# Attention of batches 2 to 7 and the states' expert rounds laid piece by piece between the batches' expert products

## The chip, the cores and the metric

The kernel runs on one core of a Trainium2 chip. Its time is the device time of one execution in microseconds (us), the median over runs. Engines are named as the profile names them: PE (TensorE), PEld (its weight loads), DVE (VectorE), ACT (ScalarE), POOL (GpSimd), SP (SyncE, which here issues loads and stores).

## The reference

Eight batches of eight heads: 512 tokens and 32 state vectors a head, 64 wide. Attention goes both ways, the tokens read the states and the states read the tokens; the two results are joined to 4352 rows of 512, and each row goes through one of eight experts, the one that its logits choose.

```python
# x (8, 8, 512, 64), state (8, 8, 32, 64), fp32
scores = scale * np.matmul(x, state.transpose(0, 1, 3, 2))       # softmax over the 32 states
xread = np.matmul(a, state)
scores2 = scale * np.matmul(state, x.transpose(0, 1, 3, 2))      # softmax over the 512 tokens
sread = np.matmul(a2, x)
attn_out = np.concatenate([xread, sread], axis=2)                # (8, 8, 544, 64)
x = attn_out.transpose(0, 2, 1, 3).reshape(B * S, H * D)         # (4352, 512)
logits = x @ w_gate                                              # w_gate (512, 8)
expert_idx = np.argmax(logits, axis=1)                           # gate_w: softmax at that index
for e in range(E):                                               # w1 (8, 512, 1024), w2 (8, 1024, 512)
    mask = expert_idx == e
    h = np.maximum(x[mask] @ w1[e], 0.0)
    out[mask] = gate_w[mask, None] * (h @ w2[e])
```

## The kernel before

All products are in fp32, which the profile shows as two passes each. The kernel has three parts in program order.

**Attention, batch by batch.** `load_x(b)` loads the tokens of a batch (three buffers `x_nat`). `transpose_x` transposes them in four groups of four through a PSUM buffer of pool `ps_m` (two buffers), each group copied to `xT` by ACT. `prep_state` (L161) transposes the states out of `bd`, a zeroed tile into which eight loads put the states block by block, into `stT`, and multiplies them with the gate weights (`pg`, to `gst`). `scores` (L183) makes `pc` (four products of 512 columns, pool `ps_c`, two buffers). `read_weights` (L191) is the softmax over the states: transpose, maximum, difference on DVE, exponential on ACT, sum and reciprocal on DVE, the scaling on POOL (L204), transpose back into `aT` on DVE (L205). `write_weights` is the softmax over the tokens: row maximum `nm` on DVE, two exponentials with sums on ACT. `transpose_write` and `write_rows` (L231) make the states' own rows (`pw`) and store them to DRAM with four small transfers that ACT issues. `logits_x` (L248) makes the tokens' logits (`pl`). The tokens' rows are never formed: `aT` stands for them.

**Routing.** `route` finds each row's expert and gate weight, `choose` (L292) the expert that most tokens of a batch want (`eb`). Batches 0 and 1 are routed after batch 1's attention, and their weights loaded then (`load_w1` L317 with one buffer, `load_w2` L321 with two); batches 2 to 7 and the states' rows are routed after the last batch. The 256 states' rows are sorted by expert into 16 groups of 32 rows, scattered to `ss_dram` by POOL at their place `slot_i` (L391, L395), and `eg` holds the expert of each group.

**Experts.** For a batch, `states_w1` (L442) multiplies the states with the expert's W1 (`pG`, to `G`), `up` (L455) applies the attention weights (`ph`, 8 x 2 products, then a relu to `hT`), and `down` (L467) multiplies with W2 in four chunks of rows (`py`, 4 x 8 products), scales them by the gate weight and stores them. So one expert serves a whole batch; tokens that want another are mended at the end under `tc.If(n_left > 0)`. The states' rows go through four **rounds** of four groups: `round_in` loads the rows (`xg`) and reads the experts' numbers into registers of SP, `round_w1` and `round_w2` load weight tiles of 1 MB by four transfers (three buffers each, `s1`, `s2`), `round_x` transposes the rows (`ptx`), `round_up` makes `pgh`, `round_h` the relu and transposes (`pth`), `round_down` makes `pgy`, `round_out` scales and scatters to the result. Half a round goes with each batch: a piece of it stands after each of the four chunks of `down`.

The source gives the order of dependent work; the framework's scheduler then lays out the order on each engine. Each engine runs its own queue strictly in that order, and SP's transfers are one such queue: a transfer that waits for a buffer holds up those behind it. All stores of the result's token rows are on SP. PSUM pools are released and allocated anew between attention and experts (L413 on), so that `ps_h` has three buffers, `ps_y` two, `ps_g` two, `ps_t` one in the second part.

```python
    for b in range(B):
        a2, s2 = soft
        if b + 2 < B:
            load_x(b + 2)
        if b + 1 < B:
            soft = weights(b + 1)
        a2T = transpose_write(a2)
        write_rows(b, a2T, s2)
        logits_x(b)
```

Of the kernel before, what the change touches and what calls it, by code (L numbers as in the profile page):

```python
# [9 lines left out]
FP32 = mybir.dt.float32  # L10
# [10 lines left out]
def kernel(  # L21
# [13 lines left out]

    nc = tc.nc
# [3 lines left out]
    DM = H * D  # L40
# [13 lines left out]
    NR = NG // 4  # L54
    FAR = 1 << 20
# [73 lines left out]

    att = tc.alloc_tile_pool(name="att", bufs=2)  # L130
    ps_c = tc.alloc_tile_pool(name="ps_c", bufs=2, space=PSUM)
    ps_m = tc.alloc_tile_pool(name="ps_m", bufs=2, space=PSUM)
    ps_o = tc.alloc_tile_pool(name="ps_o", bufs=1, space=PSUM)
# [3 lines left out]
    bd = att.tile([128, B, 2, 4, D], FP32, bufs=1)  # L137
    nc.gpsimd.memset(bd[:], 0.0)
    for i in range(4):
        for g in range(2):  # L140
            nc.scalar.dma_start(out=bd[ts(i, NS), :, g, i, :],
                                in_=state[:, 4 * g + i].rearrange("b n d -> n b d"))
# [18 lines left out]
    def prep_state(b):  # L161
        pt = ps_m.tile([128, 2, 2, 128], FP32, tag="m", name="pt")
        for j in range(NPR):
            nc.tensor.transpose(pt[:, j // 2, j % 2, :], bd[:, b, j // 2, ts(j % 2, 2), :], ident[:])  # L164
        for i in range(2):
            evict(stT[:, b].rearrange("p (g i) n -> p g i n", i=2)[:, :, i, :], pt[:, :, i, ts(i, 2 * NS)])

        pg = ps_s.tile([128, 2, E], FP32, tag="s", name="pg")
        for j in range(NPR):
            nc.tensor.matmul(pg[ds(64 * (j % 2), 64), j // 2, :], lhsT=stT[:, b, j, :], rhs=wg[:, j, :],  # L170
                             start=True, stop=True, skip_group_check=True)
        evict(gst[:, b], pg[:])

    def transpose_x(b):
        xT = att.tile([128, NPR, NC, 128], FP32, tag="xT", name="xT")
        for j in range(NPR):
            pt = ps_m.tile([128, NC, 128], FP32, tag="m", name="pt")
            for c in range(NC):
                nc.tensor.transpose(pt[:, c, :], x_nat[b][:, c, ts(j, 2), :], ident[:])  # L179
            nc.scalar.copy(xT[:, j], pt[:])  # L180
        return xT
# [49 lines left out]
    def write_rows(b, a2T, s2):  # L231


        pw = ps_o.tile([128, 2, 2, D], FP32, tag="o", name="pw")
# [90 lines left out]
    def weights(b):  # L325
        xT = transpose_x(b)
        prep_state(b)
        pc = scores(b, xT)
        read_weights(b, pc)
        return write_weights(pc)  # L330
# [3 lines left out]
    soft = weights(0)  # L334
    for b in range(B):
        a2, s2 = soft
        if b + 2 < B:
            load_x(b + 2)
        if b + 1 < B:
            soft = weights(b + 1)  # L340
        a2T = transpose_write(a2)
        write_rows(b, a2T, s2)
        logits_x(b)
        if b == 1:
            route(0, 2 * NC)
            choose(0, 2)
            for i in range(2):
                e = expert_of(eb, i)
                if i == 0:
                    load_w1(0, e)  # L350
                load_w2(i, e)
    logits_s()
    route(2 * NC, (B - 2) * NC + NST)
    choose(2, B - 2)
# [57 lines left out]
    for pool in (ps_s, ps_o, ps_m, ps_c, att):  # L412
        pool.release()  # L413


    ffn = tc.alloc_tile_pool(name="ffn", bufs=2)
    ps_h = tc.alloc_tile_pool(name="ps_h", bufs=3, space=PSUM)
    ps_y = tc.alloc_tile_pool(name="ps_y", bufs=2, space=PSUM)
    ps_g = tc.alloc_tile_pool(name="ps_g", bufs=2, space=PSUM)
    ps_t = tc.alloc_tile_pool(name="ps_t", bufs=1, space=PSUM)  # L420

    def no_dep(d):
        tc.declare_no_dep(d.ins, group="y", reason="every row of the result is written once")
        tc.add_to_no_dep_group("y", d.ins)

    def relu(dst, src):
        turn[0] += 1
        if turn[0] % 2:
            nc.scalar.activation(dst, src, AF.Relu)  # L429
        else:  # L430
            nc.vector.tensor_scalar(dst, src, 0.0, None, ALU.max)  # L431

    def scaled(dst, src, by):
        turn[0] += 1
        if turn[0] % 2:
            nc.scalar.activation(dst, src, AF.Copy, scale=by)  # L436
        else:
            nc.vector.tensor_scalar(dst, src, by, None, ALU.mult)  # L438

    gs, hs = {}, {}  # L440

    def states_w1(w1t, st):  # L442

        G = ffn.tile([128, 2, F], FP32, tag="G", bufs=1, name="G")
        for g in range(2):
            for k in range(2):
                pg = ps_h.tile([128, 512], FP32, tag="h", name="pG")
                for i in range(2):
                    j = 2 * g + i
                    nc.tensor.matmul(pg[ts(i, 64), :], lhsT=st[:, j, :], rhs=w1t[:, j, ts(k, 512)],  # L450
                                     start=True, stop=True, skip_group_check=True)
                evict(G[:, g, ts(k, 512)], pg[:])
        return G

    def up(G, a, insert=None):  # L455
        hT = [ffn.tile([128, S], FP32, tag="hT", bufs=12, name="hT") for _ in range(NFC)]
        for f in range(NFC):
            ph = ps_h.tile([128, S], FP32, tag="h", name="ph")
            for g in range(2):
                nc.tensor.matmul(ph[:], lhsT=G[:, g, ts(f, 128)], rhs=a[:, g, :],  # L460
                                 start=(g == 0), stop=(g == 1))
            relu(hT[f][:], ph[:])
            if insert:
                insert(f)
        return hT

    def down(hT, w2t, store, insert=None):  # L467
        for c in range(NC):
            py = ps_y.tile([128, DM], FP32, tag="y", name="py")
            for f in range(NFC):  # L470
                nc.tensor.matmul(py[:], lhsT=hT[f][:, ts(c, 128)], rhs=w2t[:, f, :],  # L471
                                 start=(f == 0), stop=(f == NFC - 1))
            store(c, py)
            if insert:
                insert(c)

    def store_batch(b):
        rows = out[ds(b * SO, S)].rearrange("(p c) f -> p c f", c=NC)

        def store(c, py):  # L480
            y = ffn.tile([128, DM], FP32, tag="y", bufs=3, name="y")
            scaled(y[:], py[:], gw[:, NC * b + c, :])
            no_dep(nc.sync.dma_start(out=rows[:, c], in_=y[:]))
        return store
# [4 lines left out]
    def round_in(r):  # L489
        xg = ffn.tile([128, XW], FP32, tag="xg", name="xg")  # L490
        nc.sync.dma_start(out=xg[:].bitcast(I32), in_=ss_dram[ts(r, 128)])
        rd[r].update(xg=xg, e=[expert_of(eg, 4 * r + q) for q in range(4)])

    def round_w1(r, k, half):
        t = ffn.tile([128, 4, 512], FP32, tag="s1", bufs=3, name="s1")
# [5 lines left out]
    def round_w2(r, f):  # L501
        t = ffn.tile([128, 4, DM], FP32, tag="s2", bufs=3, name="s2")
# [5 lines left out]
    def round_x(r):  # L508
# [3 lines left out]
        xT = ffn.tile([128, NDC, 128], FP32, tag="sxT", name="sxT")  # L512
        evict(xT[:], pt[:])
        rd[r]["xT"] = xT
        rd[r]["ph"] = [ps_g.tile([128, 512], FP32, tag="g", name="pgh") for _ in range(2)]
# [8 lines left out]
    def round_h(r):  # L524
        h = ffn.tile([128, F], FP32, tag="sh", bufs=1, name="sh")
        for half in range(2):
            relu(h[:, ts(half, 512)], rd[r]["ph"][half][:])
        hT = ffn.tile([128, NFC, 128], FP32, tag="shT", bufs=1, name="shT")
# [5 lines left out]
        rd[r].update(hT=hT, py=ps_g.tile([128, DM], FP32, tag="g", name="pgy"))  # L534
# [7 lines left out]
    def round_out(r):  # L542
        xg = rd[r]["xg"]
        y = ffn.tile([128, DM], FP32, tag="y", bufs=3, name="ys")
        scaled(y[:], rd[r]["py"][:], xg[:, DM:DM + 1])
# [3 lines left out]

    G = states_w1(w1s[0], stT[:, 0])  # L550
    e_next = expert_of(eb, 1)
    load_w1(1, e_next)
    round_in(0)
    hT = up(G, aT[:, 0])
    for b in range(B):
        r = b // 2
        if b % 2 == 0:
            round_x(r)
            for k in range(NDC):
                for half in range(2):  # L560
                    round_w1(r, k, half)
        else:
            round_h(r)
            for f in range(NFC):
                round_w2(r, f)
            if r + 1 < NR:
                round_in(r + 1)
        if b + 1 < B:
            G = states_w1(w1s[b + 1], stT[:, b + 1])
        if b + 2 < B:  # L570
            e = expert_of(eb, b + 2)
            load_w1(b + 2, e)
            load_w2(b + 2, e)

        def insert(c):
            if b % 2 == 0:
                round_up(r, c)
            else:
                round_down(r, 2 * c)
                round_down(r, 2 * c + 1)  # L580
        down(hT, w2s[b], store_batch(b), insert)
        if b % 2:
            round_out(r)
        if b + 1 < B:
            hT = up(G, aT[:, b + 1])
# [71 lines left out]
    for pool in (ps_t, ps_g, ps_y, ps_h, ffn):  # L657
        pool.release()
# [30 lines left out]
```

## Time and profile before

| what | us |
|---|---|
| median of three runs | 604.9 (603.94 to 605.38) |
| the profiled execution | 603.11 |
| its span | 601.3 |
| PE busy in the span | 544.4 |
| DVE, ACT, POOL busy | 137.5, 97.9, 26.9 |
| loads of the rounds' weights (s) | 256 of 256 KB |
| loads of w1t and w2t | 8 and 8 of 2048 KB |

The page divides the span into 40 slices of 15 us and gives the busy share of each engine in tenths, the clock that TensorE was granted, and the share of the 16 DMA engines. Products appear with the name of their PSUM tile first (`py<-w2t,hT` is a product into `py`). The costliest groups on PE are `py` (512 passes, 228.4 us), `ph` (256, 113.1), `pG` (128, 35.7), `pgh` and `pgy` (256 each, 30.8 each) and `pc` (64, 28.1); passes overlap in the array, so that their mean durations (599 ns for py) are longer than the time from one to the next, which a chain of many passes shows. The chain of waits follows the work that ended last back to its start; a stretch ("windows") gives sums between two times.

### The profile page before, as it was taken

The page shows a single profiled execution, that of the slowest core. Times are in us where ns is not written, and L with a number is a line of the kernel's source. Part 1 is how long each engine was busy: PE and PEld are TensorE (multiplying, and loading weights), DVE is VectorE, ACT ScalarE, POOL GpSimd, SP SyncE. Part 2 cuts the span into 40 slices and gives each one's busy share as a digit, 9 for nine tenths or more (in the row PEclk, how much of TensorE's full clock was granted, in tenths as well). Part 3 has the DMA queues.
Part 4 walks back from the last instruction along what each step waited for, and adds up shares of the span by engine and source line. Part 5 has one row for each costly group of instructions (what it writes and reads, how often), then busy time and mean ns, then how long its engine had stood idle before and what let it go on. Part 6 is the DMA issues. An engine that isn't in the chain of part 4 may idle for free.

```text
span 601.3 us, 6244 instructions
## 1 busy us (share of the span) xinstructions
PE 544.4 (91%) x2229; PEld 248.0 (41%) x2229; DVE 137.5 (23%) x255; ACT 97.9 (16%) x185; POOL 26.9 (4%) x30
## 2 busy tenths in 40 slices
PE   3796768769499999999999999999999999999996
PEld 1455546536243344334333433443343334334432
DVE  3368455544421012001100200120011002001100
ACT  1444324132111011001101100110011012001100
POOL 3021001111010000000000000000000000000000
PEclk9987878688599999999999999999999999999999
DMA  9333964000076897479488926965891888486173
GB/s 216 99 75 82 374 165 114 3 4 9 19 258 218 268 320 265 157 259 367 162 252 311 345 87 255 365 231 195 274 391 68 284 301 311 137 250 242 34 282 107
DMA packets 94513, 122.63 MB, mean 204 GB/s; under 512 B 43791, under 2 KB 43791, under 8 KB 94480
## 3 DMA queue, kind: packets, MB, share of 16 engines
q1 hardware_dynamic: 88160, 119.04, 60.0%
q10 hardware_dynamic: 5840, 2.12, 1.5%
q0 software_dynamic: 480, 1.05, 0.4%
q8 instruction: 18, 0.29, 0.2%
q14 instruction: 15, 0.12, 0.1%
HBM read 111.17 MB, written 11.54 MB: 204 GB/s over the span
## 4 chain that ended last, share of the span: by engine, by line
issue 54%; PE 30%; DVE 6%; DMA 3%; POOL 2%; ACT 2%; ACTq 1%; SPq 0%; POOLq 0%
PE py L471 9%; PE ph L460 5%; PE pc L187 4%; PE pG L450 2%; PE pw L238 2%; PE pl L252 2%; POOL sx L204 2%; DMA bd<-in_state_dram 1%; PE pgy L538 1%; ACTq L245 1%; PE pgh L520 1%; DVE aT L205 1%; PE pt L227 1%; DVE sm L201 1%; PE pg L170 1%
## 5 line engine op out<-in xcount | busy, mean ns | idle before, releaser
L471 PE MATMUL py<-w2t,hT 128*128 128x512 f32 x512 | 228.4, 599 | 0.0
L471 PEld LDWEIGHTS py<-w2t,hT 128*128 128x128 f32 x512 | 94.7, 190 | 132.4 <-issue 132.4
L460 PE MATMUL ph<-aT,G 128*128 128x512 f32 x256 | 113.1, 600 | 0.0
L460 PEld LDWEIGHTS ph<-aT,G 128*128 128x128 f32 x256 | 48.5, 192 | 65.4 <-issue 59.0
L438 DVE TENSOR_SCALAR y<-py,gw 128x512 f32<-128x512 f32 x16 | 12.0, 750 | 258.4 <-PE py L471 241.3
L436 ACT ACTIVATE y<-py,gw 128x512 f32<-128x512 f32 x16 | 11.0, 687 | 195.3 <-PE py L471 195.3
L431 DVE TENSOR_SCALAR hT<-ph 128x512 f32<-128x512 f32 x32 | 22.1, 691 | 88.5 <-PE ph L460 88.5
L450 PE MATMUL pG<-w1t,stT 128*64 128x512 f32 x128 | 35.7, 625 | 1.6 <-ACT G L125 1.6
L429 ACT ACTIVATE hT<-ph 128x512 f32<-128x512 f32 x32 | 19.1, 597 | 89.0 <-PE ph L460 89.0
L179 PE MATMUL pt<-ident,x_nat 128*128 128x128 f32 x128 | 21.2, 309 | 12.8 <-ACT xT L180 6.9
L520 PE MATMUL pgh<-s,sxT 128*32 128x512 f32 x256 | 30.8, 598 | 0.0
L538 PE MATMUL pgy<-s,shT 128*32 128x512 f32 x256 | 30.8, 598 | 0.0
L187 PE MATMUL pc<-xT,stT 128*64 128x512 f32 x64 | 28.1, 895 | 0.0
L179 PEld LDWEIGHTS pt<-ident,x_nat 128*128 128x128 f32 x128 | 15.6, 155 | 18.3 <-ACT xT L180 9.0
L546 POOL DMA_INDIRECT out_dram<-ys,xg x4 | 3.9, 980 | 426.4 <-ACT ys L436 318.1
L180 ACT COPY xT<-pt 128x512 f32<-128x512 f32 x32 | 17.5, 590 | 24.1 <-PE pt L179 14.0
L204 POOL TENSOR_TENSOR sx<-sx,sm 128x1024 f32<-128x1024 f32 x8 | 15.3, 1911 | 123.0 <-DVE sm L203 105.5
L164 PE MATMUL pt<-ident,bd 128*128 128x128 f32 x32 | 7.1, 360 | 13.9 <-DMA bd<-in_state_dram 7.6
L170 PE MATMUL pg<-wg,stT 128*64 128x8 f32 x64 | 7.0, 248 | 13.0 <-DVE stT L127 12.7
L238 PE MATMUL pw<-x_nat,a2T 128*64 128x128 f32 x256 | 17.2, 284 | 0.0
L238 PEld LDWEIGHTS pw<-x_nat,a2T 128*64 128x64 f32 x256 | 15.0, 142 | 2.7 <-issue 2.6
L450 PEld LDWEIGHTS pG<-w1t,stT 128*64 128x64 f32 x128 | 9.4, 140 | 16.2 <-issue 14.2
(117 smaller groups left out, 285.8 us busy)
## 6 DMA issues: line engine op xcount, KB each, us to landing
s<-in_moe_w_dram SPq DMA_DIRECT2D x256, 256.0 KB, 5.0
w1t<-in_moe_w_dram SPq DMA_DIRECT2D x8, 2048.0 KB, 9.5
w2t<-in_moe_w_dram SPq DMA_DIRECT2D x8, 2048.0 KB, 11.1
x_nat<-in_x_dram SPq DMA_DIRECT2D x32, 256.0 KB, 4.1
out_dram<-y SPq DMA_DIRECT2D x32, 256.0 KB, 3.0
ss_dram<-blank ACTq DMA_DIRECT2D x4, 257.0 KB, 4.4
xg<-ss_dram SPq DMA_DIRECT2D x4, 257.0 KB, 5.5
bd<-in_state_dram ACTq DMA_DIRECT2D x8, 64.0 KB, 3.9
```

The costliest lines, as they stand in the source:

```text
L179: nc.tensor.transpose(pt[:, c, :], x_nat[b][:, c, ts(j, 2), :], ident[:])
L180: nc.scalar.copy(xT[:, j], pt[:])
L187: nc.tensor.matmul(pc[ts(j % 2, 64), j // 2, :], lhsT=stT[:, b, j, :], rhs=xT[:, j], start=True, stop=True, skip_group_check=True)
L204: nc.gpsimd.tensor_tensor(sx[:], sx[:], sm[:].to_broadcast([128, NB, NS]), ALU.mult)
L238: nc.tensor.matmul(pw[ts(i, 64), g], lhsT=a2T[:, g, c, ts(i, 64)], rhs=x_nat[b][:, c, ts(2 * g + i, 2), :], start=(c == 0), stop=(c == NC ...
L429: nc.scalar.activation(dst, src, AF.Relu)
L431: nc.vector.tensor_scalar(dst, src, 0.0, None, ALU.max)
L450: nc.tensor.matmul(pg[ts(i, 64), :], lhsT=st[:, j, :], rhs=w1t[:, j, ts(k, 512)], start=True, stop=True, skip_group_check=True)
L460: nc.tensor.matmul(ph[:], lhsT=G[:, g, ts(f, 128)], rhs=a[:, g, :], start=(g == 0), stop=(g == 1))
L471: nc.tensor.matmul(py[:], lhsT=hT[f][:, ts(c, 128)], rhs=w2t[:, f, :], start=(f == 0), stop=(f == NFC - 1))
L520: nc.tensor.matmul(rd[r]["ph"][half][ts(q, 32), :], lhsT=rd[r]["xT"][:, k, ts(q, 32)], rhs=rd[r][1, k, half][:, q, :], start=(k == 0), sto ...
L538: nc.tensor.matmul(rd[r]["py"][ts(q, 32), :], lhsT=rd[r]["hT"][:, f, ts(q, 32)], rhs=rd[r][2, f][:, q, :], start=(f == 0), stop=(f == NFC ...
```

## The change

The pools of the expert part (`ffn`, `ps_h`, `ps_y`) are allocated before attention, so that both parts can stand side by side; PSUM is shared out anew: `ps_h` two buffers, `ps_y` two, `ps_c` one, `ps_m` one, `ps_s` one (`pw` uses it too). Later `ps_g` has two and `ps_t` one.

The attention of a batch is cut into pieces, as Python generators: `front(b)` yields after each of the four transpose groups, after `prep_state`, and after scores and softmax; `back(b)` yields after the transposes of the write weights, after `write_rows`, after `logits_x`. `run` advances `front(b + 1)` and `back(b)` in step, and `finish(b)` routes: batch 0, batch 1 and batch 2 alone, 3 and 4 after batch 4, 5 to 7 and the states' rows after batch 7. Attention of batches 0 and 1 runs in front; from then on `up` and `down` call `piece()` after each of the eight chunks of `up` and after each pair of products of `down`, first for the attention of batches 2 to 7 (in the expert products of batches 0 and 1 and the `up` of batch 2), then, from the `down` of batch 2 on, for the four rounds.

```diff
+    S1B, S2B = 4, 3
...
-    bd = att.tile([128, B, 2, 4, D], FP32, bufs=1)
-    nc.gpsimd.memset(bd[:], 0.0)
-    for i in range(4):
-        for g in range(2):
-            nc.scalar.dma_start(out=bd[ts(i, NS), :, g, i, :],
-                                in_=state[:, 4 * g + i].rearrange("b n d -> n b d"))
+    st2 = att.tile([128, B * 2, 2, D], FP32, bufs=1)
+    st_rows = state.rearrange("b (g i) n d -> (i n) (b g) d", g=2)
+    for u in (slice(0, 2), slice(2, 2 * B)):
+        for k in range(2):
+            nc.scalar.dma_start(out=st2[:, u, k, :], in_=st_rows[:, u])
+    nc.vector.memset(stT[:], 0.0)
...
     def prep_state(b):
-        pt = ps_m.tile([128, 2, 2, 128], FP32, tag="m", name="pt")
-        for j in range(NPR):
-            nc.tensor.transpose(pt[:, j // 2, j % 2, :], bd[:, b, j // 2, ts(j % 2, 2), :], ident[:])
+        pt = ps_m.tile([128, 2, 2, 2, NS], FP32, tag="m", name="pt")
+        for g in range(2):
+            nc.tensor.transpose(pt[:, g], st2[:, 2 * b + g], ident[:])
         for i in range(2):
-            evict(stT[:, b].rearrange("p (g i) n -> p g i n", i=2)[:, :, i, :], pt[:, :, i, ts(i, 2 * NS)])
+            evict(stT[ts(i, 64), b].rearrange("p (g j) n -> p g j n", g=2)[:, :, :, ts(i, NS)],
+                  pt[ts(i, 64), :, :, i, :])
...
+    def front(b):
+        xT = att.tile([128, NPR, NC, 128], FP32, tag="xT", bufs=1, name="xT")
+        for j in range(NPR):
+            transpose_x(b, xT, j)
+            yield
+        prep_state(b)
+        yield
+        pc = scores(b, xT)
+        soft[b] = write_weights(pc)
+        read_weights(b, pc)
+        yield
+
+    def back(b):
+        yield
+        yield
+        yield
+        a2, s2 = soft[b]
+        a2T = transpose_write(a2)
+        yield
+        write_rows(b, a2T, s2)
+        if b + 3 < B:
+            load_x(b + 3)
+        yield
+        logits_x(b)
+        yield
+
+    def finish(b):
+        b0, nb = {0: (0, 1), 1: (1, 1), 2: (2, 1), 4: (3, 2), B - 1: (5, 3)}.get(b, (0, 0))
+        if b == B - 1:
+            logits_s()
+        if nb:
+            route(b0 * NC, nb * NC + (NST if b == B - 1 else 0))
+            choose(b0, nb)
...
+    def attention(b0, b1):
+        yield from front(b0)
+        for b in range(b0, b1):
+            yield from run(*([front(b + 1)] if b + 1 < b1 else []), back(b))
+            finish(b)
...
     def up(G, a, insert=None):
-        hT = [ffn.tile([128, S], FP32, tag="hT", bufs=12, name="hT") for _ in range(NFC)]
+        hT = [ffn.tile([128, S], FP32, tag="hT", bufs=NFC, name="hT") for _ in range(NFC)]
...
     def down(hT, w2t, store, insert=None):
         for c in range(NC):
             py = ps_y.tile([128, DM], FP32, tag="y", name="py")
             for f in range(NFC):
                 nc.tensor.matmul(py[:], lhsT=hT[f][:, ts(c, 128)], rhs=w2t[:, f, :],
                                  start=(f == 0), stop=(f == NFC - 1))
+                if insert and f % 2 and f + 1 < NFC:
+                    insert()
             store(c, py)
...
         def store(c, py):
             y = ffn.tile([128, DM], FP32, tag="y", bufs=3, name="y")
-            scaled(y[:], py[:], gw[:, NC * b + c, :])
-            no_dep(nc.sync.dma_start(out=rows[:, c], in_=y[:]))
+            nc.scalar.activation(y[:], py[:], AF.Copy, scale=gw[:, NC * b + c, :])
+            no_dep(nc.scalar.dma_start(out=rows[:, c], in_=y[:]))
...
+    for _ in attention(0, 2):
+        pass
+    e0 = expert_of(eb, 0)
+    load_w1(0, e0)
+    load_w2(0, e0)
+    load_w2(1, expert_of(eb, 1))
+    work = attention(2, B)
...
+    def batch(b):
+        nonlocal G, hT
+        if b + 1 < B:
+            G = states_w1(w1s[b + 1], stT[:, b + 1])
+            if 0 < b and b + 2 < B:
+                load_w1(b + 2, expert_of(eb, b + 2))
+        down(hT, w2s[b], store_batch(b), piece)
+        if b + 2 < B:
+            e = expert_of(eb, b + 2)
+            if b == 0:
+                load_w1(b + 2, e)
+            load_w2(b + 2, e)
+        if b + 1 < B:
+            hT = up(G, aT[:, b + 1], piece)
+
+    G = states_w1(w1s[0], stT[:, 0])
+    load_w1(1, expert_of(eb, 1))
+    hT = up(G, aT[:, 0], piece)
+    batch(0)
+    batch(1)
+    for _ in work:
+        pass
...
+    def fetch(n1, n2):
+        for _ in range(n1):
+            if need1:
+                round_w1(*need1.pop(0))
+        for _ in range(n2):
+            if need2:
+                round_w2(*need2.pop(0))
+
+    def rounds():
+        round_in(0)
+        fetch(S1B, S2B)
+        for r in range(NR):
+            round_x(r)
+            yield
+            if r + 1 < NR:
+                round_in(r + 1)
+            yield
+            for k in range(NDC):
+                round_up(r, k)
+                fetch(2, 0)
+                yield
+                yield
+                yield
+            round_h(r)
+            yield
+            for f in range(NFC):
+                round_down(r, f)
+                fetch(0, 1)
+                yield
+                yield
+            round_out(r)
+
+    work = rounds()
+    for b in range(2, B):
+        batch(b)
+    for _ in work:
+        pass
```

The rounds' weight tiles have four (`s1`) and three (`s2`) buffers; `need1` and `need2` list them in order of use, and `fetch` asks for the next ones as a piece releases theirs. The scaling of the rounds' rows (`round_out`) is put on DVE alone.

## The prediction

> **What bounds the kernel now.** I read the page's forty slices first, then the sums by stretch, then the chain of waits, then the timelines of SP and POOL. The slices:
>
> ```profile
> PE   3796768769499999999999999999999999999996
> PEclk9987878688599999999999999999999999999999
> DMA  9333964000076897479488926965891888486173
> ```
>
> From slice 12 on (15 us each) TensorE is full at full clock; before it, it is a half to nine tenths busy at a lower clock, and in slices 8 to 11 the DMA engines do nothing. The stretches say how far apart the two halves are (columns: stretch, its length, busy us and instructions of PE, PEld, DVE, ACT, POOL, granted clock, DMA share, GB/s):
>
> ```profile
> 72.00:164.50 92.50, 63.48 (x458) 44.70 (x458) 46.09 (x100) 26.30 (x57) 9.55 (x5) 0.77 0.25 65
> 164.50:597.00 432.50, 431.56 (x1442) 170.38 (x1440) 52.67 (x77) 46.35 (x75) 5.07 (x5) 1.00 0.71 243
> 220.00:225.00 5.00, 5.00 (x13) 2.23 (x12) 0.77 (x2) 0.97 (x2) 0.00 (x0) 1.00 1.03 393
> 275.00:280.00 5.00, 5.00 (x13) 2.20 (x12) 0.85 (x2) 0.88 (x2) 0.98 (x1) 1.00 1.03 385
> ```
>
> The second stretch can only shrink by fewer products. The first is a chain, one batch after another (chain of waits, start, us, what):
>
> ```profile
> 60.23 3.51 PE pc L187 x7
> ...
> 64.60 1.90 PE pw L238 x32
> 66.50 1.88 PE pl L252 x16
> ...
> 72.36 1.23 DVE sm L201
> ...
> 74.33 1.92 POOL sx L204
> 76.27 1.25 DVE aT L205
> 77.52 0.19 DVE stT L127
> ```
>
> Scores, softmax through VectorE, ScalarE and GpSimd, and only then the next batch's state copy and scores: aT L205 ends at 77.5 and at 110.5 two batches later, 16.5 us a batch here, 18.3 for the next (128.8). The later stage goes at these rates:
>
> ```profile
> 179.55 0.44 PE ptx L511 x4
> 179.99 3.58 PE pG L450 x16
> 183.57 7.06 PE py L471 x16
> 190.63 1.85 PE pgh L520 x16
> ...
> 219.24 13.93 PE ph L460 x32
> ```
>
> **What the change removes: the exposed attention of batches 2 to 7.** I price TensorE's work behind the first product with W1 (pG), at full clock. Experts and rounds: py 512 x 0.441 = 225.9; ph 256 x 0.435 = 111.4; pG 128 x 0.224 = 28.7; pgh and pgy 512 x 0.116 = 59.3; 48 transposes of rounds x 0.11 = 5.3; sum 430.6. (The stretch above has 431.6, so the rates hold.) In the built program's order, what stands behind the first pG of attention is batches 4 to 7 whole, batch 3 from its last score product on and batch 2's pw and pl: 64 transposes of x, 40 of weights, 8 of states at 0.11 = 12.3; pc 34 x 0.224 (its shape is pG's) = 7.6; pw 6 x 1.90 = 11.4; pl 6 x 1.88 = 11.3; pg 4 x 0.5 = 2.0; the states' logits and counts 3.8. Sum 48.4, together **479.0**.
>
> The clock is part of this: pc takes 0.50 a pass in the chain (3.51/7), where the clock is 0.77, and pG of the same shape 0.224 at 1.00.
>
> **Where the products start.** The same order puts them behind batch 3's first three score products. Walk: x of batch 0 has landed at 7.3 as now. With one buffer for transposes in place of two, each group goes 0.54 for four transposes, 0.58 for the copy (L180) and two handoffs of 0.2: 1.5, so the fourth copy ends near 13; the states wait no longer for the 3.5 us memset (L138) and its eight loads (18.0 now), so states 1, pg 0.5 and eight score passes at 0.5 end at 18 (now 23.7). Softmax 0 takes its 13.9 (23.7 to 37.6 now) plus about 1.5, as the row maximum and its wait for two exponentials now stand ahead of the transpose on VectorE; the scores of batch 1 end at 35.5. Softmax 1 with batch 0's routing in its queue: 15.5, so 51. Batch 2's scores stand on TensorE behind batch 1's logits (1.9) and around its count (route 2): 58.5. Then six transpose groups 9.0, exponential and state 1.6, three score pairs at the cold 0.49 x 6 = 2.9: **72**. Expert 0 is known at about 50 (57.9 now) and its 2 MB take 9.5 (w1t, page), so weights do not set this start. If the softmaxes overlap better 66, if every handoff doubles 78.
>
> **What it adds behind the start.**
> - Cold first products: now ph's first 32 take 15.0 against 13.9, and 162.5 to 164.5 has clock 0.50. I take 2.5 (1 to 3.5).
> - Two buffers for pG and ph, where there were three: an eviction (0.59 or 0.69) and two handoffs just exceed a pG group of 0.9. 0.2 x 8 = 1.5 (0 to 4). If ScalarE is late, ph waits too; that is in the next term.
> - Attention among products. Per batch there are seven pieces between products of 4 x 0.441, 12.3, and 8.9 of its own, 21.2 us of TensorE, against the chain's 17 or so plus the evictions, relus and the y scaling now in the same queues (1 to 5 us). It nearly fits. Nothing in this trace shows such a mixture. Lower bound 0 (TensorE has more work than the chain is long), upper 14 (5 us late, less 2, times five batches). 6, nearer to the row of 17.
> - The states' last rows: their load now stands on SP behind batch 3's w2 (2 MB). TensorE has 9 us of ph to cover 8.7; 1 (0 to 2).
> - The rounds' start. Now the scatter, the first rows and the first weights are hidden under 15 us of ph:
>
> ```profile
> 165.40 1.14 POOL L395 DMA_INDIRECT ss_dram<-srow,slot_i  x1 [20.92 <-DVE slot_i L391]
> ...
> 174.19 0.34 SPq L491 DMA_DIRECT2D xg<-ss_dram  x1
> 175.04 8.54 SPq L497 DMA_DIRECT2D s<-in_moe_w_dram  x12
> ```
>
> The place index is ready at 165.1, the rows' load is issued 9.1 later, weights 9.9 later, and four loads of 256 KB need about 2 to issue and 5.0 to land: 17. In the changed order only eleven py (9.7) and two short pieces (1.3) stand in between, and SP's weights are queued behind the waiting rows. 17 + 0.9 - 11 is **7** (3 to 9).
> - Weights in the rounds. Between the first ptx and the last pgy TensorE has 286 us of work (same sums). In it go 67.1 MB of s, 16.8 of w1t and w2t, 7.3 of outputs: 91 MB, 318 GB/s. The rows above reach 385 to 393, so 236 us would do, but leads are short: three s2 tiles have 7 us between the release of their buffer and their use, against 2 + 5 to issue and land; the input of round 3 waits on SP for round 1's scatter and a 2 MB w2 stands ahead of its weights. 5 (0 to 18).
> - The y stores move from SP to ScalarE's queue. Their loads (0.35 each on SP) leave SP; on ScalarE a store waits for its y and, in the built program, for an earlier transfer that shares its semaphore, and relus queue behind it. TensorE's py and ph buffers cover about 2 us; without that each late transfer would show whole. Counted in the 5.
> - All y on ScalarE, ys on VectorE, state loads of two instead of eight shapes, the memset of stT: nothing, since 0.69 per 7 us of py hides the first two, and the memset ends (1.8, half of the 3.5 of L138) before the first state copy at 13. Uncovered, that memset would cost 1.8 once.
> - The tail: now the last product ends at 596.1 and the span at 601.3, with an indirect store last. Then y (0.7), issue and landing 3.0: 4.5 (4 to 5).
>
> **The sum.** 72 + 479.0 + 2.5 + 1.5 + 6 + 1 + 7 + 5 + 4.5 = 578.5 of span. The profiled execution took 603.1 against its span of 601.3, so 580.3; the median of the runs is 1.8 above that execution, which makes **582**.
>
> The Trainium skill, "TensorE: Matmul & The Clock Gate", part 1 on the clock gate, says that idling longer than some 3.4 us returns the array to half clock for about as long again; the rows agree with half clock (0.50 against 0.224 a pass). By it the 7 us wait at the rounds' start costs 1.7 more and the total were 584. The skill's "DMA: Bandwidth & Descriptors", section on the specifications, speaks against the change's denser loading: it limits a core to about 358 GB/s from HBM. The rows of 385 and 393 deny it, and by it 91 MB would take 254 us, still under 286, with the same sum.
>
> **Rivals.**
> - *The gaps close* (0.18): handoffs overlap as in the later stage today (431.6 busy of 432.5). Start 66, terms 1, 0.5, 1, 0, 3, 1, tail 4.3: 555.8 + 3.6 = 559. Against it: the first stage today idles at one buffer more.
> - *The softmax chain sets the pace* (0.14): 25 us a batch against 21.2, five batches, 19 instead of 6: 595, with a late start 601. For it: stT of the next batch stands behind aT on VectorE, in the new order too. Against: TensorE has more work than the chain's 17.
> - *Loading sets the rounds' pace* (0.15, slower): place, the weights of the rounds with four and three buffers and one in-order SP. At 270 GB/s, between 243 over the stage now and 318 asked, 91 MB take 337, so 51 in place of 5: 628. It decides below 91/(286 + 5 + 23) = 290 GB/s. For it: a short lead, and a late load holds up all behind it. Against: 385 and 393 in stretches of weights alone.
> - *The moved work isn't overlapped* (0.03): the order still runs attention in front, 603 to 607. The order speaks against it.
>
> **Numbers.** The forecast, 570 to 596, has 0.50. About 0.2% is what a measurement tells from no change. Faster: 0.50 + 0.18 + 0.13 = 0.81; same 0.03; slower 0.16. The range for 8 in 10, 558 to 610, leaves out half of the first rival and most of the third.
>
> **What would show it.** pG of batch 0 first at 66 to 78 and not behind a w1 load; py, ph at 0.441 and 0.435 with attention between; pc at about 0.22 a pass; slices near 9 from the fifth on; one gap of 3 to 9 at the first ptx; DMA over 300 GB/s in the rounds, with idle on TensorE before pgh or pgy under 10 us in all. I am wrong if TensorE's idle behind the start exceeds 43 us (20.5 in the sum and the 23 that are lacking to 605), or if its products slow down.

## The result and the profile after

The changed kernel is slower: 642.94 us median (642.71 to 645.0) against 604.42 (602.91 to 605.38), a ratio of 1.065 with a 95% interval of 1.062 to 1.068. Its profiled span is 640.8 us. The prediction said 582, with 558 to 610 as its range.

The page's slices after (16 us each here):

```profile
PE   1778699999999999799999999999999999999997
PEclk9996799999999999999999999999999999999999
DMA  9433930376131044976985879677697779635501
```

The picture is the one that was predicted. From the sixth slice on TensorE is full at full clock, but for the slice in which the rounds start, where before it was so from the twelfth or thirteenth. The sums by stretch (length; busy us and count of PE, PEld, DVE, ACT, POOL; granted clock; DMA share; GB/s) say how full, first for the attention among products, then for the rounds:

```profile
81.00:240.00 159.00, 156.96 (x765) 81.33 (x763) 62.65 (x123) 44.81 (x89) 10.85 (x6) 1.00 0.34 106
270.00:636.00 366.00, 364.50 (x1124) 114.55 (x1121) 28.59 (x41) 37.53 (x60) 3.91 (x4) 1.00 0.69 236
```

TensorE idles 2.0 us in the first and 1.5 in the second. So hardly anything waits, and yet the kernel is slower: the work itself has grown. The costliest groups show where (tile, passes | busy us, mean ns of one):

```profile
L429 PE MATMUL py<-w2t,hT 128*128 128x512 f32 x512 | 241.8, 606 | 0.0
L418 PE MATMUL ph<-aT,G 128*128 128x512 f32 x256 | 123.3, 609 | 0.0
L581 PE MATMUL pgh<-s,sxT 128*32 128x512 f32 x256 | 60.3, 602 | 0.0
L599 PE MATMUL pgy<-s,shT 128*32 128x512 f32 x256 | 59.5, 604 | 0.0
```

The rounds' products in the kernel before:

```profile
L520 PE MATMUL pgh<-s,sxT 128*32 128x512 f32 x256 | 30.8, 598 | 0.0
L538 PE MATMUL pgy<-s,shT 128*32 128x512 f32 x256 | 30.8, 598 | 0.0
```

pgh and pgy were busy 30.8 us each and are now busy 60.3 and 59.5, with the same 256 passes each and the same mean duration. Only the time from one to the next can have changed. Two stretches of TensorE's timeline, before and after (start, length, what, how many passes; a product in fp32 is two passes). Before:

```profile
183.50 7.13 PE L471 MATMUL py<-w2t,hT 128*128 128x512 f32 x16
190.56 1.93 PE L520 MATMUL pgh<-s,sxT 128*32 128x512 f32 x16
192.42 7.13 PE L471 MATMUL py<-w2t,hT 128*128 128x512 f32 x16
```

After:

```profile
265.51 1.05 PE L581 MATMUL pgh<-s,sxT 128*32 128x512 f32 x2
266.49 1.13 PE L429 MATMUL py<-w2t,hT 128*128 128x512 f32 x2
267.54 1.04 PE L581 MATMUL pgh<-s,sxT 128*32 128x512 f32 x2
268.52 1.12 PE L429 MATMUL py<-w2t,hT 128*128 128x512 f32 x2
...
317.01 2.78 PE L599 MATMUL pgy<-s,shT 128*32 128x512 f32 x22
319.72 2.84 PE L418 MATMUL ph<-aT,G 128*128 128x512 f32 x6
```

Before, eight products of pgh stand together, and from their start to the next py is 1.86 us: 0.116 a pass. After, one product (x2) stands between two of py, and a pair of one pgh and one py takes 267.54 - 265.51 = 2.03 us. The py alone is 2 x 0.441 = 0.88, so the lone pgh adds 1.15 us, 0.58 a pass. The last two lines show the same kind of product still at 0.123 a pass (2.71 us from the first to the next product) where eleven stand together. A pgh or pgy product fills 32 of the array's 128 columns (the shape `128*32`), its quarter given by q; four quarters side by side share the time of one full pass, and a full-width product between them seems to end that.

In the changed kernel's order on TensorE, pgh and pgy stand in 101 runs between full-width products: 41 of one product, 28 of two, 8 of three, 15 of four, 8 of eight and one of eleven. Before there were 32 runs of eight. The source suggests why: each weight tile comes by four transfers, one a quarter, so that the scheduler can expect a quarter's product ahead of its neighbours' and fill up with py. No run here tests that; what follows tests the order itself.

### The profile page after: what moved, and what is told of

Read it like the earlier page. It is cut to its first block, busy times and chain, and to the rows that moved or that the text cites. A ratio compares the mean times of both kernels' runs of the same rounds, so it can differ in the third digit from the quotient of the medians.

```text
span 640.8 us, 6269 instructions
## 1 busy us (share of the span) xinstructions
PE 600.3 (94%) x2225; PEld 235.7 (37%) x2225; DVE 131.6 (21%) x287; ACT 108.9 (17%) x202; POOL 23.4 (4%) x29
## 4 chain that ended last, share of the span: by engine, by line
PE 85%; issue 6%; ACT 4%; DMA 3%; DVE 2%; ACTq 1%; SPq 0%; POOL 0%; POOLq 0%
PE py L429 33%; PE ph L418 16%; PE pgh L581 9%; PE pgy L599 8%; PE pG L408 4%; PE pc L193 4%; PE pt L186 3%; PE pw L244 2%; PE pl L258 2%; PE pt L233 1%; DMA st<-in_state_dram 1%; ACT xT L187 1%; DMA ss_dram<-srow,slot_i 1%; ACT a L221 1%; PE pth L593 1%
## 5 line engine op out<-in xcount | busy, mean ns | idle before, releaser
L429 PE MATMUL py<-w2t,hT 128*128 128x512 f32 x512 | 241.8, 606 | 0.0
L418 PE MATMUL ph<-aT,G 128*128 128x512 f32 x256 | 123.3, 609 | 0.0
L581 PE MATMUL pgh<-s,sxT 128*32 128x512 f32 x256 | 60.3, 602 | 0.0
L442 ACT ACTIVATE y<-py,gw 128x512 f32<-128x512 f32 x32 | 22.0, 687 | 224.2 <-PE py L429 200.6
L599 PE MATMUL pgy<-s,shT 128*32 128x512 f32 x256 | 59.5, 604 | 0.0
L186 PE MATMUL pt<-ident,x_nat 128*128 128x128 f32 x128 | 26.3, 333 | 20.7 <-ACT xT L187 12.1
L581 PEld LDWEIGHTS pgh<-s,sxT 128*32 128x32 f32 x256 | 9.4, 108 | 42.0 <-issue 32.8
L599 PEld LDWEIGHTS pgy<-s,shT 128*32 128x32 f32 x256 | 8.6, 108 | 37.7 <-issue 33.1
L258 PEld LDWEIGHTS pl<-gst,aT 128*128 128x128 f32 x128 | 15.2, 194 | 5.8 <-issue 5.3
L233 PE MATMUL pt<-ident,a 128*128 128x128 f32 x64 | 12.0, 319 | 4.2 <-ACT a2T L234 2.0
```

The source lines that it names most:

```text
L258: nc.tensor.matmul(pl[:, c, :], lhsT=aT[:, b, g, ts(c, 128)], rhs=gst[:, b, g, :], start=(g == 0), stop=(g == 1), skip_group_check=True)
L442: nc.scalar.activation(y[:], py[:], AF.Copy, scale=gw[:, NC * b + c, :])
L581: nc.tensor.matmul(rd[r]["ph"][half][ts(q, 32), :], lhsT=rd[r]["xT"][:, k, ts(q, 32)], rhs=rd[r][1, k, half][:, q, :], start=(k == 0), sto ...
L599: nc.tensor.matmul(rd[r]["py"][ts(q, 32), :], lhsT=rd[r]["hT"][:, f, ts(q, 32)], rhs=rd[r][2, f][:, q, :], start=(f == 0), stop=(f == NFC ...
```

## Experiments

**Grouped.** The changed kernel with the four quarters of a group kept together, the one that is loaded last first:

```diff
+    def together(one):
+        last = one(3)
+        with tc.issue_after(last.ins):
+            for q in range(3):
+                one(q)
...
-            for q in range(4):
-                nc.tensor.matmul(rd[r]["ph"][half][ts(q, 32), :], ...)
+            def one(q):
+                return nc.tensor.matmul(rd[r]["ph"][half][ts(q, 32), :], ...)
+            together(one)
```

> The changed kernel with one edit: the four products of a quarter group (pgh or pgy, q = 0 to 3) are issued with nothing between them, q = 3 first. In the changed kernel its 512 pgh and pgy passes are busy 119.8 us, in the kernel before 61.6. Theory (the loss is the overlap of the four quarter-width products, which ends where a full-width product stands between them): one run of such products between full-width ones takes about 1.15 us whether it holds one or two (period 2.03 us for one pgh and one py, less 0.88 for the py), and at most 1.15 for four; 39 runs of four, 5 shorter or longer and 9 of eight to twelve make 61 to 71 us, so 49 to 58 us go and the time is 585 to 594. Rival (the loading of the rounds' weights or the y stores on ScalarE's queue hold the products up, and the longer pgh only shows the wait): the time stays above 630. Rival (half and half: with the stage 50 us shorter the same 67 MB of weights don't come in time): 600 to 625, with idle before pgh and pgy over 10 us.

Measured: 593.27 us, 0.983 of the kernel before (0.979 to 0.987). 49.7 us are gone, and the sign of the change is turned by the order of 256 products alone. Its groups:

```profile
L581 PE MATMUL pgh<-s,sxT 128*32 128x512 f32 x256 | 33.6, 601 | 3.1 <-DMA s<-in_moe_w_dram 3.1
L600 PE MATMUL pgy<-s,shT 128*32 128x512 f32 x256 | 37.0, 603 | 1.6 <-DMA s<-in_moe_w_dram 1.6
```

119.8 us have become 70.6, 49.2 less; the time follows to within 0.5. The rivals wanted over 630, or 600 to 625 with more than 10 us of idle before these products; there are 4.7.

**Ones, twos and fours.** The other direction: the kernel before, with nothing changed but where its rounds' products stand. `PIECE` is 1, 2 or 4:

```diff
             for f in range(NFC):
                 nc.tensor.matmul(py[:], lhsT=hT[f][:, ts(c, 128)], rhs=w2t[:, f, :],
                                  start=(f == 0), stop=(f == NFC - 1))
+                if insert and f % PIECE == PIECE - 1:
+                    insert(c, f + 1 - PIECE, f + 1)
             store(c, py)
-            if insert:
-                insert(c)
```

> The kernel before, its rounds' products laid one by one behind each py product, in place of eight behind eight py; loads, buffers and everything else as before. Theory (a full-width product between quarter-width ones ends their overlap): 256 runs of 1.15 us in place of 32 of 1.85: 294 less 59, 235 us more, 840 us (800 to 860). Rival (the changed kernel's loss comes from loading or queues): the work is the same and the time stays within 590 to 620.

> As the run of ones, with two rounds' products behind every two py. Theory: 128 runs of 1.15 (two quarters still overlap each other): 147 less 59, 88 us more, 692 us (670 to 710). If two quarters in a row did not overlap, 840 as with ones. Rival (loading or queues): 590 to 620.

> As the run of ones, with four rounds' products (one whole quarter group) behind every four py. Theory: 64 runs of 0.93 to 1.15 us: 60 to 74 less 59, 0 to 15 us more, 604 to 620. It tells whether a single group of four already has the full overlap or needs a second group behind it. Rival (loading or queues): no change, 600 to 608, here not told apart from the lower end.

Measured: ones 841.29 us, 1.393 of before (1.383 to 1.404); twos 686.71, 1.137 (1.132 to 1.143); fours 613.75, 1.017 (1.013 to 1.022). All three lie where the theory put them, and 237 us appear in a kernel whose loads, queues and buffers are as they were. Timelines of ones, of twos and of fours:

```profile
201.88 1.04 PE L522 MATMUL pgh<-s,sxT 128*32 128x512 f32 x2
202.85 1.12 PE L472 MATMUL py<-w2t,hT 128*128 128x512 f32 x2
203.91 1.04 PE L522 MATMUL pgh<-s,sxT 128*32 128x512 f32 x2
```

```profile
201.61 1.98 PE L472 MATMUL py<-w2t,hT 128*128 128x512 f32 x4
203.52 1.05 PE L522 MATMUL pgh<-s,sxT 128*32 128x512 f32 x4
204.51 1.98 PE L472 MATMUL py<-w2t,hT 128*128 128x512 f32 x4
```

```profile
205.16 1.07 PE L522 MATMUL pgh<-s,sxT 128*32 128x512 f32 x8
206.15 3.70 PE L472 MATMUL py<-w2t,hT 128*128 128x512 f32 x8
209.78 1.06 PE L522 MATMUL pgh<-s,sxT 128*32 128x512 f32 x8
```

One pgh run of four products takes hardly longer than one of two, or of one. The price of a run, from its period less 0.882 for each py:

| products in a run | period us | the run us | runs | time by 604 + runs - 59.5 | measured |
|---|---|---|---|---|---|
| 1 | 2.03 | 1.15 | 256 | 839 | 841.3 |
| 2, two quarters | 2.90 | 1.14 | 128 | 690 | 686.7 |
| 4, four quarters | 4.62 | 1.10 | 64 | 615 | 613.8 |
| 8, each quarter twice (before) | 8.92 | 1.86 | 32 | 604 | 603.9 |

**Twos on one quarter.** Is that a fixed price of a run, or an overlap of quarters? The run of twos, with the two products of each pgh run on the same quarter:

```diff
-            half, q = i // 4, i % 4
+            q, half = i // 2, i % 2
```

> The run of twos (686.7 us), with the two products of each pgh run on the same quarter (both halves of one q) in place of two quarters; pgy's runs stay as they were. It tells a fixed price of a run apart from an overlap of quarters. Theory (a quarter takes its own passes one after another at 0.44, only different quarters overlap): a run of two is 4 x 0.44 and 0.2, 1.96 us, in place of 1.14; 64 runs, 52 us more: 739 us (725 to 750). Rival (a run of up to four products has a fixed price of some 1.1 us, whichever quarters): 683 to 690.

Measured: 746.7 us (741.57 to 751.14), 1.234 of before (1.223 to 1.244). The run now takes 206.45 - 202.70 - 1.76 = 1.99 us in place of 1.14:

```profile
202.70 1.98 PE L472 MATMUL py<-w2t,hT 128*128 128x512 f32 x4
204.62 1.90 PE L522 MATMUL pgh<-s,sxT 128*32 128x512 f32 x4
206.45 1.98 PE L472 MATMUL py<-w2t,hT 128*128 128x512 f32 x4
```

So the price of a run isn't fixed. A quarter takes its own passes one by one at the 0.44 us of a full-width pass, different quarters run side by side, and a run costs 0.44 for each pass of its fullest quarter. By the table 0.1 to 0.3 is left over in each run, which goes with the change from full width to quarters and back.

**Quarter by quarter.** The kernel before, with a run of eight in the order q0, q0, q1, q1, ... in place of q0 to q3 twice (the two loops of `round_up` exchanged).

> The kernel before with the eight products of a group of pgh in the order quarter by quarter (q0 of both halves, q1 of both, ...) in place of half by half; the same work and the same runs of eight. It asks what overlaps in a run. If each quarter of the array takes its own passes and only the run matters: no change, 602 to 606. If neighbours must be of different quarters to overlap: four passes of one quarter in a row take 4 x 0.44 and only the ends overlap, a run 5.7 us in place of 1.85, 16 runs, 62 us more: 655 to 670.

Measured: 604.52 us, 1.004 (1.000 to 1.007). Exchanging the order within a run made no difference that counts (a run 1.87 us in place of 1.86); what the run holds does. The exchange did reach the engine: in the trace the first passes of the four quarters now start 13 ns apart, before 7, which fits two products of a quarter issued in a row.

**Eights.** The grouped kernel with both halves of a k, or two f, in one run; so that two tiles are there at once, `s2` gets a fourth buffer. The rounds' pools are also released ahead of the branch at the end.

```diff
-    S1B, S2B = 4, 3
+    S1B, S2B = 4, 4
...
-            for f in range(NFC):
+            for f in range(0, NFC, 2):
                 round_down(r, f)
-                fetch(0, 1)
+                fetch(0, 2)
...
```

> The grouped kernel (593.3 us) with eight products of the rounds together in place of four (both halves of a k, or two f), a fourth s2 buffer, and the weight buffers given back ahead of the branch at the end. Theory (a run between full-width products costs some 0.2 us beside 0.85 to 0.93 for each overlapped four): 25 runs of eight, 3 of four and 3 longer make 60 us against the 70.6 that the grouped kernel's pgh and pgy are busy: 11 us less, 582 us (578 to 587). Rival (a group of eight has to wait for the later of two tiles' loads, eight of 256 KB): the 11 us come back as idle before pgh and pgy, 590 to 600.

Measured: 585.52 us, 0.971 (0.968 to 0.973), 7.8 less than grouped. Its groups:

```profile
L581 PE MATMUL pgh<-s,sxT 128*32 128x512 f32 x256 | 31.0, 599 | 1.2 <-DMA s<-in_moe_w_dram 1.2
L602 PE MATMUL pgy<-s,shT 128*32 128x512 f32 x256 | 30.4, 598 | 1.8 <-DMA s<-in_moe_w_dram 1.8
```

pgh and pgy are busy as before the change, 9.2 less than grouped. The rival's wait takes no more than 3.0 us (idle before them). This kernel is the change with the rounds' products at their old price. So the rest of the change is worth 18 us, and the scattering cost 57 net (642.9 less 585.5); the fourth buffer and the earlier release are in that difference and were not run alone.

**ScalarE's queue.** The start was late too: the first pG at 81.0. ScalarE's timeline in the changed kernel and in one with eight issues moved to GpSimd:

```profile
1.28 4.41 ACTq L148 DMA_DIRECT2D st<-in_state_dram  x4
6.35 6.18 ACTq L157 DMA_DIRECT2D ss_dram<-blank  x4
12.56 1.28 ACT L187 ACT_TABLE_LOAD   x1 [12.56 <-DMA st<-in_state_dram]
13.85 0.58 ACT L187 COPY xT<-pt 128x512 f32<-128x512 f32 x1
```

```profile
1.28 1.28 ACT L187 ACT_TABLE_LOAD   x1 [1.28 <-PEq L748]
7.72 0.58 ACT L187 COPY xT<-pt 128x512 f32<-128x512 f32 x1 [5.15 <-PE pt L186]
9.51 0.59 ACT L187 COPY xT<-pt 128x512 f32<-128x512 f32 x1 [1.21 <-PE pt L186]
```

```diff
-            nc.scalar.dma_start(out=st2[:, u, k, :], in_=st_rows[:, u])
+            nc.gpsimd.dma_start(out=st2[:, u, k, :], in_=st_rows[:, u])
...
-        nc.scalar.dma_start(out=ss_dram[ts(r, 128)], in_=blank[:])
+        nc.gpsimd.dma_start(out=ss_dram[ts(r, 128)], in_=blank[:])
```

> The grouped kernel with the eight loads and stores that stand at the head of ScalarE's queue (st2 and the blanks of ss_dram) issued by GpSimd. In the changed kernel the first copy of xT starts at 13.85, behind 10.6 us of these issues, where the transposes it waits for end at 9.8. Theory (ScalarE's queue holds the head up): xT's fourth copy ends 4 us earlier and the first pG starts at 76 to 78 in place of 80.4; time 3 to 4.5 us less, 589 to 590.5. Rival (the softmax chain on VectorE and the routing of batch 0 set the start): pG at 79 to 81, 592 to 594.

Measured: 587.91 us, 0.973 (0.969 to 0.977), 5.4 less than grouped and a little more than expected; the first pG at 74.8 in place of 80.4. Against grouped the first copy starts 5.7 us earlier (7.72 in place of 13.38), and the start gains 5.6 of it. ScalarE's queue had held the copy 3.6 us after its transposes were done at 9.8; the other 2.1 are the tokens of batch 0, whose last transfer lands earlier here (the fourth transpose starts at 7.2 in place of 9.3). The profiled execution, 590.96, was the longest of four (584.43 to 590.96): behind its start TensorE idles 1.1 us more than in grouped and is busy 2.4 more, so the 5.4 rests on the medians.

**Buffers of the head.** The grouped kernel with py's two PSUM buffers lent to the transposes of batches 0 to 2.

```diff
+    def pt_tile(b, shape):
+        spare[0] += 1
+        if b < 3 and spare[0] % 3:
+            return ps_y.tile(shape, FP32, tag="y", name="pt")
+        return ps_m.tile(shape, FP32, tag="m", name="pt")
...
-            pt = ps_m.tile([128, NC, 128], FP32, tag="m", name="pt")
+            pt = pt_tile(b, [128, NC, 128])
```

> The grouped kernel with three PSUM buffers in place of one for the transposes of x and of the weights of batches 0 to 2 (the two of py, which stand empty until the products start). With one buffer a group of four takes 1.80 us (1.12 of transposes, 0.68 until the copy is done). Theory (the one buffer sets the head): ten groups on the chain of the head at 0.5 to 0.7 less, first pG at 74 to 76, time 587 to 589. Rival (softmax or ScalarE's copies set it): pG at 79 to 81, 592 to 594.

Measured: 582.17 us, 0.966 (0.961 to 0.972), 11.1 less than grouped, more than expected. The first pG is at 73.7, 6.7 earlier; TensorE's idle behind the start is about 2 us less (7.8 against 9.7). The remaining 2 are TensorE's busy time behind the start (495.4 against 497.3) and were not traced further.

**y stores on SP.** The grouped kernel with the stores of y issued by SP again (`nc.sync` in place of `nc.scalar` in `store_batch`).

> The grouped kernel (593.3 us) with the stores of y issued by SP again, as in the kernel before, in place of ScalarE. If the stores on ScalarE's queue cost nothing, since TensorE is full: 591 to 595. If a store that waits there holds relus and with them TensorE's buffers up (part of the 5 us that the prediction gave to the weights in the rounds): 2 to 5 us less, 588 to 591. If on SP the waiting stores hold the rounds' loads up: 597 to 610.

Measured: 589.85 us, 0.976 (0.973 to 0.980), 3.4 less than grouped; TensorE no longer waits for weights before pgh and pgy (4.7 us in the grouped kernel), and behind the start it idles 3.2 us in all in place of 9.7. So the loads on SP did not suffer. That the time fell by less than the idle is in part the clock, granted at 0.66 from 260 to 265, where grouped has 1.00.

**All three.** Eights, three buffers for the transposes of batches 0 to 3, and the eight issues on GpSimd; then the same with y on SP.

> The runs of eight, the three buffers (now for batches 0 to 3) and the eight issues on GpSimd in one kernel. Theory (the three are separate terms: grouping 7.8 of work, the buffers 11.1 and the queue 5.4 of the head, the last two partly the same wait): 582.2 less 7.8, less 3 to 5.4, less 2 for batch 3's groups: 567 to 570, with the first pG at 63 to 70. Rival (the start is then held by the first expert's 2 MB, issued once batch 0 is counted, 55.3 in the run with three buffers, and landing 9.6 later): pG not before 62 to 65 even so, which with a queue 5 us earlier is 60. Rival (the rounds' loading now sets the pace, at 91 MB in some 300 us): 575 to 582.

> The best kernel so far (568.2 us) with the stores of y issued by SP in place of ScalarE. In the grouped kernel that took 3.4 us off. If the same waits are there: 564 to 566. If TensorE is as full without (idle of 5.6 us behind the start, in all, in the best kernel): 566 to 569. If SP's waiting stores now hold the denser loads up: 570 to 580.

Measured: 568.19 us, 0.944 of before (0.940 to 0.948), with the first pG at 64.3, inside the expectation; with y on SP 566.16, 0.936 (0.930 to 0.942), not told apart from it. The 5.6 us of idle in the last expectation leave out the rounds; with them it is 9.0 in the first of the two. Its stretch of the rounds:

```profile
256.00:560.00 304.00, 300.56 (x1105) 113.71 (x1104) 28.60 (x41) 36.73 (x59) 3.88 (x4) 1.00 0.80 279
```

## Why the prediction was wrong, step by step

The span was predicted at 578.5 and is 640.8, 62.3 more: 9.0 of start, 67.6 of work behind it (549.1 busy against 479.0 and 2.5), less 13.6 of stalls that didn't come (6.9 against 20.5) and 0.7 of tail.

*The step that failed* is "pgh and pgy 512 x 0.116 = 59.3". They measured 119.8: 60.5 us, nearly the whole miss. The 0.116 came from a row of sixteen passes in one run, and such a duration belongs to the pass with its neighbours. The prediction took the order of the built program for attention and for the start, but priced the rounds as if their runs stayed whole. With the table above, the order alone gives it: 92 runs of one to four at about 1.14, 8 of eight at 1.86 and one of eleven at some 2.6 make 122 us. The prediction's own condition for being wrong, "or if its products slow down", is what happened; no rival had it. There is a rule on it that was not weighed: the Trainium skill, "TensorEngine Tiling (Array Packing)", section Tiling Modes, says that changing the tiling mode, not just the tile, drains TensorE. No run here shows a drain by itself; what could hold one is the 0.1 to 0.3 us that a run takes beyond its fullest quarter's passes. The larger part is that a lone product streams for 0.88 us while three quarters stand empty, where in company its share is 0.23.

*The start*, 72, was 81.0, outside 66 to 78. A group of transposes was put at 1.5 and takes 1.80 with one buffer; three buffers give 6.7 back. The tokens of batch 0 had landed at 9.3, not "at 7.3 as now". And the walk let the first copy of xT run when its transposes were done, though ScalarE's queue first issues eight transfers, which in the kernel before stand behind the first two copies (8.74): "the fourth copy ends near 13" was 19.8, and 13.7 once these issues were moved.

*Py, ph and cold products.* The rate of py held where its products stand in a run: the last seventeen passes take 7.46 us, 0.44 each. Outside pgh and pgy TensorE was busy 429.3 us behind the start, against 422.2 predicted with the cold 2.5; grouped it is 426.7. Where the rest of this difference lies was not traced.

*The stalls* were priced too high, but for one. The two buffers for pG and ph: 1.5 predicted, nothing measured before pG. Attention among products: 6 predicted, 0.95 measured. The states' last rows: 1 predicted, 1.1 measured. The rounds' start: 7 predicted, 3.3 measured. Weights in the rounds: 5 predicted, and no idle before pgh or pgy in the changed kernel; the 1.5 us of idle from 270 on stand before pth, which waits for the relu. In the best kernel, where the loads run denser, 3.4 are idle there, 1.1 of them for weights. The tail was put at 4.5, though its own two terms, 0.7 and 3.0, make 3.7; from the end of the last product at 637.05 it was 3.8.

*The clock.* The 1.7 us that the prediction named as lost behind the wait at the rounds' start don't show in the changed kernel, whose granted clock is 1.00 from 240 to 270. But they show in five of the kernels derived from it: in eights, in the one with ScalarE's issues moved and in the one with y on SP the granted clock is 0.66 in the 5 us around the end of that wait (3.1, 3.4 and 2.2 us long), which is 5 x 0.34 = 1.7; with three buffers and in the best kernel it comes to the same over 10 us. Grouped, with a wait of 2.7, keeps 1.00. So the loss is real, but the length of the wait alone doesn't tell whether it comes.

*The rivals.* "The gaps close" came nearest for the stalls: 5.5 us in its terms, 6.9 measured. "The softmax chain sets the pace" and "the moved work isn't overlapped" fall by the 2.0 us of idle in 81 to 240. "Loading sets the rounds' pace" had the right sign and the wrong cause: it would have shown as idle before pgh and pgy, and there is none at 236 GB/s in the changed kernel and 1.1 us at 279 in the best. Loading was not the limit, and 0.16 for slower was too little because the one price that the change could alter on TensorE itself was taken as fixed.

With the products kept in eights the span is 584.8, 6.3 above the 578.5 of the sum: 7.8 of late start and 9.2 of work, less 10.0 of stalls and 0.7 of tail. The rest of the sum was near because its errors cancel, not because each term was right.

## What to carry to other kernels

A duration from a profile holds with the neighbours it was measured beside: before narrow products are spread out as fillers, look how long their runs become in the new order, and price runs, not passes. Quarter-width products are cheap only in runs that hold all four quarters, better twice over; if a scheduler fills gaps with them, tie a run together behind the one whose input comes last. An engine that is full and yet later than planned is a sign to compare the busy time of each group, not the waits.

## What the runs showed of the hardware

- A lone quarter-width product between full-width ones adds 1.15 us, four different quarters together 1.10, two products of one quarter 1.99 (fp32, two passes of 512 columns each).
- Within a run of eight, two products of one quarter in a row did not delay the other quarters: 604.5 us against 603.5 for the other order.
- Eight transfers at the head of ScalarE's queue kept its first copy, whose transposes ended at 9.8 us, waiting to 13.85, at 1.1 us an issue for the first four and 1.5 for the rest.
- Behind a wait of TensorE of 2.2 us (y on SP) the granted clock was 0.66 in the 5 us from its end, behind one of 3.3 us (changed kernel) 1.00.
